# RWKV-7 recurrence and a SoLU block on one core: inverted blocks issued ahead of four loads, parts of an inverse moved behind evictions, the last store on two queues

## The chip, the cores and the metric

The kernel runs on one core of one Trainium2 chip. The metric is the device time of one execution in microseconds (us), as the median of seven runs. Engines: TensorE (PE; PEld are its weight loads), VectorE (DVE), ScalarE (ACT), GpSimd (POOL) and SyncE (SP), which here only issues DMAs. Each engine works through its instructions strictly in the order in which the program gives them.

## The reference

```python
B, H, S, D = 4, 8, 768, 40          # r, k, v, w, a, b: (B, H, S, D), float32
state = zeros(B, H, D, D)
for t in range(S):
    y[:, :, t] = einsum('bhd,bhde->bhe', r_t, state)
    Sa    = einsum('bhde,bhe->bhd', state, a_t)
    state = state * w_t[:, :, None, :] - einsum('bhd,bhe->bhde', Sa, b_t)
    state = state + einsum('bhd,bhe->bhde', v_t, k_t)
x = y.transpose(0, 2, 1, 3).reshape(B * S, H * D)      # 3072 x 320
h = x @ w_in                                           # w_in 320 x 1024, float64
solu = h * softmax(h)
out = (layernorm(solu) * g_ln) @ w_out                 # w_out 1024 x 320, float64
```

## The kernel before

**Tiling.** The sequence is cut into 12 rounds of 64 time steps (`L = 64`, `NCH = 12`). A round is one set of loads: for each of w, b, a, k, v and r two DMAs of 64 partitions with 16 runs of 160 bytes each. A round has two steps `i` (`N = 24` in all), each with two of the four batches and all eight heads. Within a step the recurrence is turned into matrix products over the 64 positions. This needs the inverse of a unit triangular 64 x 64 matrix for every batch and head.

**The inverse.** For the first four rounds (`FINE = 4`) only the 16 x 16 diagonal blocks are inverted by elimination; TensorE puts them together to 32 and 64. The blocks travel through DRAM so that every partition holds one block:
- `scatter(n)` (L424) writes the blocks of round n to DRAM with four DMAs of 512 runs of 128 bytes;
- `gather(n)` (L434) reads them back with two DMAs;
- `invert_fine(n)` is the elimination on VectorE: one step sets up u (L447, L448), fourteen steps are a product and a subtraction each (L456, L458; called pairs 1 to 14 here), the last copies u on ScalarE (L462) and writes it to DRAM with two DMAs (L464);
- `bring_inverse(n)` (L499) reads u back into the tile tinvT, two steps at a time, with four DMAs of 512 runs of 128 bytes;
- `solve(i)` transposes tinvT on VectorE (L598) and builds the larger inverse: py on TensorE, its eviction to `y_16` on VectorE (L602), pz on TensorE, evictions to tinvT on ScalarE (L613, or L610 for step 0), then py, y_mid, pz and L633 for the last doubling.

Step 0 takes another way: `solve(0)` doubles the blocks from 1 to 16 on TensorE, with L589 and the transpose L593 on VectorE and a copy on ScalarE (L592) at each doubling, while `invert(0)` works beside it for step 1.

**Other parts of a step.** `front(i)` makes decays and keys: the logarithm of w (L353), inv (L358), the products with b and k on GpSimd (L360), transposed a and b (L400, L401, L289) and the triangular matrix nt (L311). `attend(i)` makes psi and lamv; its fourth part transposes r (prT, L289). `recurrence(i)` makes pu, nuT, lamu, the output pyo and the next state sm; `readout(i)` makes x (L730). After a round, `repack` (L741 to L744) brings x into xT with twelve DMAs. From step 6 on, `hidden` and `output` compute the SoLU block for the step six behind; every second step ends in `store(n)` with two DMAs. `weights()` (W) brings in the matrices of the SoLU block piece by piece over GpSimd's queue (L228) and narrows them from 64-bit floats (the tile bits) on VectorE and ScalarE (L179 to L191).

**The order.** It is written out by hand. In `turns(order, ...)` each letter stands for the next part of one of these generators: f and g are fronts, r recurrence, a attend, s solve, I the inverse of the round to come, y readout, X repack, B the arrivals, W weights, L a later load, `*` a filler matmul. Where a letter I stands for several steps, a list says how many; for the step `i` that is `inverse_steps(i)`. `EARLY[1]` is the order of step 0 alone, `EARLY[0]` that of steps 1 to 5. Before the loop, two strings of letters cover the fronts of steps 0 to 3 and `solve(0)`.

**Queues.** Nearly all DMAs are issued by SyncE, one behind the other, and each may wait for the data it moves, for the readers of its target, and for the DMA that is eight places ahead of it. Between steps 0 and 1 the program issues, in this order: `scatter(2)`, k of round 3, r of round 1, and then, in the part B of step 1, `bring_inverse(1)` and `gather(2)`. k of round 3 is first read by GpSimd in the front of step 6, r of round 1 by prT in step 1.

```python
            if js and js[-1] % 2:
                scatter(js[-1] // 2)
            if i == 0:
                load(3, "k")
                load(1, "r")
            begin(i + 1)
```

Of the kernel before, what the change touches and what calls it, by code (L numbers as in the profile page):

```python
# [19 lines left out]
L = 64  # L20
# [36 lines left out]
def doubling_masks():  # L57

    s, t = np.arange(P)[:, None] % L, np.arange(L)[None, :]
    return np.concatenate([(s // (2 * b) == t // (2 * b)) & (s & b == 0) & (t & b != 0) for b in (1, 2, 4, 8)],  # L60
                          1).astype(np.float32)
# [3 lines left out]
def kernel(  # L65
# [28 lines left out]
    nc = tc.nc  # L94
# [4 lines left out]
    NCH = S // L  # L99
# [176 lines left out]
    def half(p):  # L276
        return slice(64 * p, 64 * p + 64)
# [41 lines left out]
    of_round = [dict() for _ in range(NCH)]  # L319

    def load(n, *names, by=(nc.sync, nc.sync)):

        if n >= NCH:
            return
        d = of_round[n]
        for name in names:
            ap = dict(w=w, b=b, a=a, k=k, v=v, r=r)[name]
            if name in "vr":
                d[name] = dict(v=v_t, r=r_t)[name][n % 2]
                to = d[name].rearrange("q s h c -> q (s h) c")[:, :, 0:D]  # L330
            else:
                d[name] = raw.tile([P, 2, H, D], FP32, tag="raw_" + name, name="raw_" + name)
                to = d[name].rearrange("q s h c -> q (s h) c")
            for c in range(2):
                by[c].dma_start(out=to[half(c)], in_=ap[2 * c:2 * c + 2, :, n * L:(n + 1) * L, :]  # L335
                                  .rearrange("b h t d -> t (b h) d"))
# [39 lines left out]
    def quarter(q):  # L376
        return slice(Q * q, Q * q + Q)

    def homes(q, steps=slice(0, 2)):

        return slice((q * 2 + steps.start) * H, (q * 2 + steps.stop) * H)
# [36 lines left out]
    def scatter(n):  # L418

        d = of_round[n]  # L420
        d["blocks"] = dram.tile([64, Q, Q], FP32, tag="blk_dram", name="blk_dram")
        nt = d["nt"].rearrange("q s p g t -> q (s p g) t")
        for q in range(4):
            nc.sync.dma_start(out=d["blocks"][homes(q)].rearrange("h s t -> s h t"),  # L424
                              in_=nt[quarter(q), :, quarter(q % 2)])

    def gather(n):


        if n < FINE:  # L430
            R = Q // 2
            nb = of_round[n]["nb"] = two.tile([P, R, R], FP32, tag="blk", name="blk", bufs=2)
            for z in range(2):
                nc.sync.dma_start(out=nb[half(z)],  # L434
                                  in_=of_round[n]["blocks"][:, R * z:R * z + R, R * z:R * z + R])
            return
        nb = of_round[n]["nb"] = two.tile([P, Q, Q], FP32, tag="blk", name="blk", bufs=2)
        for p in range(2):
            nc.sync.dma_start(out=nb[half(p)], in_=of_round[n]["blocks"])
# [55 lines left out]
    def bring_inverse(n, steps=slice(0, 2)):  # L495

        u = of_round[n]["u"]
        for q in range(4):
            nc.sync.dma_start(  # L499
                out=ti_t[quarter(q), steps, :, :, quarter(q % 2)].rearrange("s z p g t -> s (z p g) t"),  # L500
                in_=u[homes(q, steps)].rearrange("h s t -> s h t"))
# [307 lines left out]
    def store(n):  # L809
        rows = out.rearrange("(b s) d -> s b d", b=B)[n * L:(n + 1) * L]  # L810
        for c in range(2):
            nc.sync.dma_start(out=rows[:, 2 * c:2 * c + 2, :], in_=of_round[n]["osb"][half(c)])

    def steps(part, n):
        for _ in range(n):
            if part:
                next(part, None)

    def turns(order, more, **parts):

        for x in order.split():
            n = more.get(x, 1)
            steps(parts.get(x), n.pop(0) if isinstance(n, list) else n)

    def fronts(i):

        return [j for j in ((4, 5) if i == 0 else (i + AHEAD,)) if j < N]

    EARLY = ("r r a r B W f I r r W I W s y r X W a I s f L W a I a s W f I a f W s I a f W s f W",
             "r r a r W f r r W g W s y r W a f g L W a I a s f g W a I s f g W I s a f g W I s f g W I")  # L830
    STEADY = "r b r a r B f b b o r o I o r o s y o r X I o h a f L a s a h f a I h f s h f h a f h"
    CENTRE = "r r a r f o I r o r o s y o r X I o h a f L a s a h I f s a h I f s h f s h I a f h"
    LATE = "r b r r a B b b r o o I o r o s y o r X I o h a L a s a h a I h s h h a h"
# [4 lines left out]
    def begin(i):  # L838
        for j in fronts(i):
            front_of[j] = front(j)  # L840
            steps(front_of[j], 1)

    def inverses():
        for n in range(1, NCH):
            yield from invert(n)

    def inverse_steps(i):

        if i == 0:
            return [5, 5, 5, 1, 0]  # L850
        if i == LAG - 1:
            return [0, 0, 4, 4, 3, 3]
        if i == LAG:
            return [3, 3, 4, 4, 4]
        if i < LAG:
            return [0, 0, 2, 2, 2, 2] if i % 2 else [3, 3, 1, 1, 0, 0]
        return [0, 7, 7] if i % 2 else [6, 7, 5]

    def warm(n, x):

        for _ in range(n):
            nc.tensor.matmul(idle[:, 0:x.shape[1]], lhsT=x[:, 0:P], rhs=x, start=True, stop=True)

    def fillers():
        while True:
            warm(1, sm_t[0].rearrange("q c g d -> q (c g d)")[:, 0:256])
            yield
# [5 lines left out]
    def arrivals(i):  # L873

        n = (i + 1) // 2
        if n < NCH:
            bring_inverse(n)
        if n + 1 < NCH:
            gather(n + 1)
        yield  # L880

    def later(n, *names):
# [3 lines left out]
    with tc.manual_schedule():  # L886
        both = (nc.sync, nc.scalar)
        load(0, "w", "b", "a", by=both)
        nc.scalar.dma_start(out=masks, in_=nc.inline_tensor(doubling_masks(), name="masks").ap())
        load(0, "k", "v")  # L890
        load(1, "w", "a", "b")
        warm(3, sm_t[0].rearrange("q c g d -> q (c g d)"))
        f, g, at, inv, so, ws = front(0), front(1), attend(0), invert(0), solve(0), weights()
        turns("f g f g f f g g f f f g g s g a", {}, f=f, g=g, s=so, a=at)
        f, g, warmer = front(2), front(3), fillers()
        scatter(0)
        load(0, "r")
        gather(0)
        load(1, "k")
        load(2, "w")  # L900
        turns("f g s f s * g a s f I s I f a s I g I s I g a I", dict(I=[2, 3, 3, 3, 3, 99]), f=f, g=g, s=so, a=at, I=inv,
              **{"*": warmer})
        load(2, "a", "b")
        bring_inverse(0, slice(1, 2))
        turns("s f W s * f a s a g s g f g W W", {}, f=f, g=g, s=so, a=at, W=ws, **{"*": warmer})
        scatter(1)
        load(2, "k")
        gather(1)
        load(1, "v")
        begin(0)  # L910
        inv = inverses()
        after, before = None, None
        for i in range(N):
            m, more, js = i - LAG, i + 1 < N, fronts(i)
            now = hidden(m) if m >= 0 else None
            parts = dict(r=recurrence(i), y=readout(i), I=inv, W=ws, h=now, b=after, o=before)
            if i == LAG:
                steps(ws, 99)
                parts["o"] = centre()
                steps(parts["o"], 1)  # L920
            parts.update(zip("fg", (front_of[j] for j in js)))
            if more:
                parts.update(a=attend(i + 1), s=solve(i + 1))
            if i % 2 == 0:
                load((i + 6) // 2, "w", "a")
                parts["L"] = later((i + 6) // 2, *("bk" if i else "b"))
            else:
                parts["X"] = repacked(i // 2)
                parts["B"] = arrivals(i)
            order = EARLY[len(js) - 1] if i < LAG else CENTRE if i == LAG else STEADY if js else LATE  # L930
            turns(order, dict(I=inverse_steps(i)), **parts)
            if i % 2:
                load((i + 3) // 2, "v", "r")
            if js and js[-1] % 2:
                scatter(js[-1] // 2)
            if i == 0:
                load(3, "k")
                load(1, "r")
            begin(i + 1)
            after, before = now, output(m) if m >= 0 else None  # L940
        for m in range(N - LAG, N):
            now = hidden(m)
            turns("b h h h h h o o h b b o o o o", {}, h=now, b=after, o=before)
            after, before = now, output(m)
        turns("b b b o o o o o o", {}, b=after, o=before)
# [30 lines left out]
```

## Time and profile before

| | |
|---|---|
| median of seven runs | 675.37 us (672.97 to 681.46) |
| profiled execution, its own time | 672.97 us |
| its span, first to last instruction | 670.9 us |
| mean granted TensorE clock | 0.976 |
| TensorE busy | 608.9 us (91% of the span) |
| VectorE busy | 443.0 us (66%) |
| ScalarE busy | 275.4 us (41%) |
| GpSimd busy | 119.5 us (18%) |
| bytes moved by DMA | 53.74 MB in 238155 packets |

All times below are counted in us from the start of the span. The profile is of one execution, the fastest of the seven. A busy TensorE is not TensorE at its peak, as the ends of its matmuls are modelled. "[1.71 <-issue]" behind an instruction is the idle time of its engine just before it and what ended it; such a cause is inferred, and a wait for several things is put down to one of them. "SPq" is SyncE issuing a DMA, "DMA x<-y" a transfer that is waited for.

### The profile page before, as it was taken

The page shows a single profiled execution, that of the slowest core. Times are in us where ns is not written, and L with a number is a line of the kernel's source. Part 1 is how long each engine was busy: PE and PEld are TensorE (multiplying, and loading weights), DVE is VectorE, ACT ScalarE, POOL GpSimd, SP SyncE. Part 2 cuts the span into 40 slices and gives each one's busy share as a digit, 9 for nine tenths or more (in the row PEclk, how much of TensorE's full clock was granted, in tenths as well). Part 3 has the DMA queues.
Part 4 walks back from the last instruction along what each step waited for, and adds up shares of the span by engine and source line. Part 5 has one row for each costly group of instructions (what it writes and reads, how often), then busy time and mean ns, then how long its engine had stood idle before and what let it go on. Part 6 is the DMA issues. An engine that isn't in the chain of part 4 may idle for free.

```text
span 670.9 us, 28595 instructions
## 1 busy us (share of the span) xinstructions
PE 608.9 (91%) x12579; PEld 428.9 (64%) x12579; DVE 443.0 (66%) x1203; ACT 275.4 (41%) x663; POOL 119.5 (18%) x219
## 2 busy tenths in 40 slices
PE   7877677888789999999999999999999999999996
PEld 4666565776666677677667767676765666555554
DVE  4459567684796786886876876976967844323423
ACT  3254545565435344434534443452443334412312
POOL 4424313322221121122112112111200100000000
PEclk9798879998999999999999999999999999999999
DMA  9769649474373546454453643654234120000000
GB/s 154 111 147 153 124 81 161 81 135 98 82 118 50 94 80 109 66 100 88 78 96 81 90 84 77 85 94 93 39 67 81 24 41 19 21 24 21 20 21 20
DMA packets 238155, 53.74 MB, mean 80 GB/s; under 512 B 227400, under 2 KB 235344, under 8 KB 238032
## 3 DMA queue, kind: packets, MB, share of 16 engines
q1 hardware_dynamic: 232928, 45.80, 40.2%
q0 software_dynamic: 1696, 5.25, 3.0%
q8 instruction: 99, 1.62, 1.1%
q10 hardware_dynamic: 3408, 0.87, 0.9%
q14 instruction: 24, 0.20, 0.1%
HBM read 36.95 MB, written 10.22 MB: 70 GB/s over the span
## 4 chain that ended last, share of the span: by engine, by line
PE 66%; DVE 13%; ACT 6%; SPq 5%; issue 5%; DMA 3%; ACTq 1%; DVEq 0%
PE po L799 16%; PE h L754 13%; PE pyo L723 4%; PE pcx L370 3%; PE plnT L794 3%; PE py L547 3%; PE pz L547 3%; PE pcum L357 2%; DVE prod L486 2%; DVE u L488 2%; PE plamv L308 2%; SPq L335 2%; PE ppsi L308 2%; DVE nmax L764 2%; PE plamu L308 2%
## 5 line engine op out<-in xcount | busy, mean ns | idle before, releaser
L754 PE MATMUL h<-w_in,xT 128*128 128x512 f32 (+1 forms) x288 | 125.0, 624 | 0.0
L799 PE MATMUL po<-w,lnT 128*128 128x320 f32 x384 | 115.9, 440 | 3.2 <-ACT lnT L795 3.2
L799 PEld LDWEIGHTS po<-w,lnT 128*128 128x128 f32 x384 | 68.3, 190 | 29.2 <-ACT lnT L795 5.8
L488 DVE TENSOR_TENSOR u<-u,prod 128x30 f32<-128x30 f32 (+7 forms) x240 | 66.6, 278 | 8.2
L486 DVE TENSOR_TENSOR prod<-blk,u 128x30 f32<-128x30 f32 (+7 forms) x240 | 65.7, 274 | 7.2 <-DMA blk<-blk_dram 0.3
L764 DVE TENSOR_REDUCE nmax<-h 128x1 f32<-128x1024 f32 x24 | 29.3, 1221 | 52.5 <-PE h L754 52.5
L360 POOL TENSOR_TENSOR kx<-raw_b,inv 128x320 f32<-128x320 f32 x24 | 21.0, 876 | 233.5 <-ACT inv L358 220.9
L754 PEld LDWEIGHTS h<-w_in,xT 128*128 128x128 f32 (+1 forms) x288 | 38.0, 188 | 29.7 <-issue 27.7
L804 ACT ACTIVATE osb<-po,rs 128x320 f32<-128x320 f32 x24 | 12.6, 527 | 98.9 <-PE po L799 82.2
L795 ACT COPY lnT<-plnT 128x512 f32<-128x512 f32 x48 | 27.0, 587 | 41.1 <-PE plnT L794 41.0
L786 POOL TENSOR_TENSOR rs<-c,mhalf 128x1 f32<-128x1 f32 x24 | 13.2, 549 | 151.7 <-DVE c L785 150.6
L311 DVE TENSOR_TENSOR lamv<-plamv,cst 128x512 f32<-128x512 f32 x24 | 16.6, 690 | 31.8 <-PE plamv L308 30.8
L771 DVE TENSOR_TENSOR e<-h,e 128x1024 f32<-128x1024 f32 x24 | 29.4, 1224 | 10.0 <-ACT e L768 9.4
L547 PE MATMUL py<-tinv,nt 32*32 32x32 f32 x1280 | 24.0, 196 | 13.1 <-DVE tinv L598 11.6
L768 ACT ACTIVATE e<-h,nmax 128x1024 f32<-128x1024 f32 x24 | 26.8, 1115 | 20.6 <-DVE nmax L764 15.3
L633 ACT ACTIVATE tinvT<-pz 32x256 f32<-32x256 f32 x48 | 17.9, 373 | 40.9 <-PE pz L547 40.6
L370 PE MATMUL pcx<-cst,lw 128*128 128x132 f32 x192 | 31.7, 290 | 2.8 <-DVE y L602 1.5
L370 PEld LDWEIGHTS pcx<-cst,lw 128*128 128x128 f32 x192 | 26.4, 192 | 11.2 <-ACT y_mid L629 3.4
L372 ACT ACTIVATE kx<-pcx 128x264 f32<-128x264 f32 x48 | 18.8, 392 | 33.1 <-PE pcx L370 32.8
L709 POOL TENSOR_TENSOR sm<-tot,fac 128x320 f32<-128x320 f32 x20 | 14.8, 740 | 96.7 <-DVE tot L708 63.0
L547 PEld LDWEIGHTS py<-tinv,nt 32*32 32x32 f32 x1280 | 20.2, 110 | 17.8 <-issue 13.9
L776 DVE BATCH_NORM_STATS2 bs<-e 128x6 f32<-128x512 f32 x48 | 30.8, 684 | 0.6
(139 smaller groups left out, 1173.0 us busy)
## 6 DMA issues: line engine op xcount, KB each, us to landing
blk<-blk_dram SPq DMA_DIRECT2D x16, 256.0 KB
raw_k<-in_k_dram SPq DMA_DIRECT2D x24, 160.0 KB
v<-in_v_dram SPq DMA_DIRECT2D x24, 160.0 KB
r<-in_r_dram SPq DMA_DIRECT2D x24, 160.0 KB
out_dram<-osb SPq DMA_DIRECT2D x24, 160.0 KB
raw_w<-in_w_dram SPq DMA_DIRECT2D x23, 160.0 KB
raw_b<-in_b_dram SPq DMA_DIRECT2D x23, 160.0 KB
raw_a<-in_a_dram SPq DMA_DIRECT2D x23, 160.0 KB
```

The source lines that it names most:

```text
L308: nc.tensor.matmul(t[half(c ^ p * cross), p, g * L:(g + 1) * L], lhsT=lhs[half(p), g, half(c)], rhs=rhs[half(p), g, half(c)], start=True, ...
L370: nc.tensor.matmul(t[:, g * 132:g * 132 + 132], lhsT=pair(lw, 2 * j + g), rhs=cst[:, lo:lo + 132], start=True, stop=True)
L486: nc.vector.tensor_tensor(out=t, in0=nb[:, j:j + 1, j + 1:Q].to_broadcast([P, rows, m]), in1=u[:, 0:rows, j:j + 1].to_broadcast([P, rows, ...
L488: nc.vector.tensor_tensor(out=u[:, 0:rows, j + 1:Q], in0=u[:, 0:rows, j + 1:Q], in1=t, op=ALU.subtract)
L547: nc.tensor.matmul(t[quarter(out), c:c + Q], lhsT=lhs(p, g), rhs=rhs(p, g), start=True, stop=True)
L723: nc.tensor.matmul(t[half(p), c, g * W:g * W + used], lhsT=kb[half(c), j, 2 * g + p, :], rhs=lam[half(c), h % 2, h // 2, 0:used], start=i ...
L754: nc.tensor.matmul(h[:, j * 512:j * 512 + 512], lhsT=of_round[i // 2]["xT"][rows, kt, i % 2 * P:i % 2 * P + P], rhs=w_in[rows, 4 if kt == ...
L764: nc.vector.tensor_reduce(out=nmax, in_=h, axis=AX.X, op=ALU.max, negate=True)
L771: nc.vector.tensor_tensor(out=q, in0=h, in1=e, op=ALU.mult)
L776: nc.vector.bn_stats(out=bs[:, j], in_=q[:, j * 512:j * 512 + 512])
L795: nc.scalar.copy(out=lnT[:, fs.start:fs.stop].rearrange("p f t -> p (f t)"), in_=t)
L799: nc.tensor.matmul(o[:, 0:DM], lhsT=lnT[:, f, :], rhs=w2[:, f, :], start=f == 0, stop=f == NF - 1)
```

## The change

Five edits:
- In `arrivals` and the loop, `load(3, "k")` and `load(1, "r")` leave their place behind `scatter(2)`. In step 1 SyncE now issues `bring_inverse(1)`, k of round 3, `gather(2)` and r of round 1, in this order.
- In the first of the two strings of letters before the loop, the parts I (the inverse of round 0) are placed anew among the parts s, and the eighth s moves from the start of the second string to the end of the first, ahead of the last I. On VectorE, the transpose that ends the second doubling then comes ahead of the setting up of u and pair 1, the one that ends the third comes after pair 7 in place of pair 10, and L602 comes ahead of pair 14 but behind pairs 8 to 13.
- In `EARLY[1]`, one s goes ahead of I: L602 for step 1 comes ahead of the setting up of u of round 1.
- `inverse_steps(0)` gives 4 and 6 steps to the first two I in place of 5 and 5.
- Of the two DMAs of the last `store`, the second is issued by ScalarE.

On TensorE and GpSimd the order of the instructions is the same in both kernels. On ScalarE only the DMA at the end is added.

```diff
     def store(n):
         rows = out.rearrange("(b s) d -> s b d", b=B)[n * L:(n + 1) * L]
         for c in range(2):
-            nc.sync.dma_start(out=rows[:, 2 * c:2 * c + 2, :], in_=of_round[n]["osb"][half(c)])
+            (nc.scalar if c and n == NCH - 1 else nc.sync).dma_start(out=rows[:, 2 * c:2 * c + 2, :], in_=of_round[n]["osb"][half(c)])
...
     EARLY = ("r r a r B W f I r r W I W s y r X W a I s f L W a I a s W f I a f W s I a f W s f W",
-             "r r a r W f r r W g W s y r W a f g L W a I a s f g W a I s f g W I s a f g W I s f g W I")
+             "r r a r W f r r W g W s y r W a f g L W a a s I f g W a I s f g W I s a f g W I s f g W I")
...
     def inverse_steps(i):
         if i == 0:
-            return [5, 5, 5, 1, 0]
+            return [4, 6, 5, 1, 0]
...
     def arrivals(i):
         n = (i + 1) // 2
         if n < NCH:
             bring_inverse(n)
+        if i == 1:
+            load(3, "k")
         if n + 1 < NCH:
             gather(n + 1)
+        if i == 1:
+            load(1, "r")
         yield
...
-        turns("f g s f s * g a s f I s I f a s I g I s I g a I", dict(I=[2, 3, 3, 3, 3, 99]), f=f, g=g, s=so, a=at, I=inv,
+        turns("f g s f s * g a s f s I f a s I g I s I I g a s I", dict(I=[2, 3, 3, 3, 3, 99]), f=f, g=g, s=so, a=at, I=inv,
               **{"*": warmer})
         load(2, "a", "b")
         bring_inverse(0, slice(1, 2))
-        turns("s f W s * f a s a g s g f g W W", {}, f=f, g=g, s=so, a=at, W=ws, **{"*": warmer})
+        turns("f W s * f a s a g s g f g W W", {}, f=f, g=g, s=so, a=at, W=ws, **{"*": warmer})
...
             if js and js[-1] % 2:
                 scatter(js[-1] // 2)
-            if i == 0:
-                load(3, "k")
-                load(1, "r")
             begin(i + 1)
```

## The prediction

> **What bounds the kernel now.** The page came first. It names TensorE, but a busy share of 91% says little about the start, so the chain of waits was read next, in pieces.
>
> ```profile
> PE 608.9 (91%) x12579; PEld 428.9 (64%) x12579; DVE 443.0 (66%) x1203; ACT 275.4 (41%) x663; POOL 119.5 (18%) x219
> PE 66%; DVE 13%; ACT 6%; SPq 5%; issue 5%; DMA 3%; ACTq 1%; DVEq 0%
> ```
>
> From 120 us on the chain runs along TensorE and its evictions in program order, with no instruction that the diff touches until the last store. What the early steps gain or lose should therefore arrive at the end undiminished. Three early places and the tail remain. The chain from 70 us (start, duration, what):
>
> ```profile
> 75.14 0.48 SPq L424
> ...
> 77.08 2.01 SPq L335
> ...
> 79.13 1.02 SPq L335
> ...
> 80.67 2.01 SPq L499
> ...
> 83.27 1.11 SPq L499
> ...
> 84.42 2.37 DMA tinvT<-u_dram
> ...
> 86.91 0.71 DVE tinv L598
> ```
>
> Here the end is set by SyncE's queue: scatter of round 2 (L424), loads of k of round 3 and r of round 1 (L335), and only then the inverted blocks (L499), whose landing starts the transpose L598. TensorE's timeline shows the price:
>
> ```profile
> 77.61 0.66 PE L289 MATMUL pvT<-cst,v 128*128 128x128 f32 x4
> 87.77 1.08 PE L547 MATMUL py<-tinv,nt 32*32 32x32 f32 x64 [9.50 <-DVE tinv L598]
> ...
> 91.02 1.11 PE L289 MATMUL prT<-cst,r 128*128 128x128 f32 x4
> ```
>
> 9.50 us idle; 3.25 us later prT reads r, one of the loads that the change puts behind. The second place, first TensorE, then VectorE:
>
> ```profile
> 58.75 0.69 PE L308 MATMUL plamv<-rT,vT 64*64 64x64 f32 x32
> 61.16 1.01 PE L547 MATMUL pz<-tinvT,y 32*32 32x32 f32 x62 [1.71 <-issue]
> ```
>
> ```profile
> 58.71 0.28 DVE L447 TENSOR_SCALAR u<-blk 128x256 f32<-128x256 f32 x1
> ...
> 60.71 0.35 DVE L602 SCALAR_TENSOR_TENSOR y<-py,cst 128x128 f32<-128x128 f32 x1
> ```
>
> The gap is called issue, but pz reads y of L602, which ends at 61.06. Its input py was done at 56.9; five steps of the inverse (from L447) stand ahead of it. The third place is alike:
>
> ```profile
> 35.91 0.44 DVE L593 STREAM_TRANSPOSE y_mid<-tinv 128x256 f32<-128x256 f32 x1
> ...
> 37.96 0.18 DVE L458 TENSOR_TENSOR u<-u,prod 128x14 f32<-128x14 f32 x1
> 38.05 0.34 DVE L602 SCALAR_TENSOR_TENSOR y<-py,cst 128x128 f32<-128x128 f32 x1
> ```
>
> ```profile
> 38.45 0.75 PE L547 MATMUL pz<-y_mid,y 32*32 32x32 f32 x64 [1.18 <-DVE y L602]
> ```
>
> VectorE works without a pause from 31.93 to 38.4 and TensorE waits for it.
>
> **Third place (20 to 45 us), inverse of round 0.** The new order takes three multiply-subtract pairs from the free time before psi (VectorE idles 30.75 to 31.25 today, and would idle from 30.2) and puts them after 32.27. Before L602 then stand pairs 2 to 13 in place of 5 to 14: pairs 2, 3, 4 added (0.40 + 0.46 + 0.46 us by their spacing at 29.45 to 30.77), pair 14 taken away (0.40). L602 is 0.9 later. The copies of u on ScalarE (0.83 at 38.17) stand ahead of the copies of tinvT (L610) and wait for pair 14, now behind L602: by 39.8 against 38.17, and L610 from 40.6 against 39.24. The chain through L615 to py (40.98) loses 1.4. Bounds: -0.7 (the transpose L593, now ahead of three pairs, had waited 0.75 after its copy at 35.16, and this is all that could be won) and +1.7. I take +1.4, since no idle time of VectorE is left to absorb the pairs.
>
> A wider TensorE gap may also cost clock. It grows from 1.18 to about 2.1 us. The granted clock (the column ahead of the last two) after the 1.71 us gap above:
>
> ```profile
> 60.00:62.00 2.00, 0.84 (x67) 0.88 (x69) 1.86 (x8) 0.00 (x0) 0.00 (x0) 0.82 1.11 205
> 62.00:64.00 2.00, 2.00 (x51) 1.61 (x39) 1.83 (x8) 0.90 (x4) 0.54 (x1) 0.50 1.15 164
> ```
>
> It stays at half until 71.5; after the other gap of this size (1.74 us at 18.6) it is half from 20.3 to 27.1. These changes, and those at 81.7 and 92.0, lie multiples of 3.41 us apart. Four paT transposes take 1.09 us at half clock and 0.63 to 0.81 at full. So a drop here is possible: two windows of 3.4 us at a rate of 1/1.55 lose 2.4 us. It needs the gap to lie well inside a window, so it stays a rival. The Trainium skill ("TensorE: Matmul & The Clock Gate", HAM oscillation) warns of idle gaps above some 3.4 us; by that rule no gap of 2.1 us would cost anything, but the rows show a fall after 1.7. By the rule the term stays +1.4, by the rows it may be +3.8.
>
> **Second place (50 to 75 us).** L602 moves from behind five steps to right after psi (ending 58.7), so pz starts when plamv ends, at 59.45: 1.71 sooner. The steps lose nothing, for VectorE is busy from 50 to 70.3 in either order. It then idles 1.47 until pnt, and TensorE's lead removes that: nt comes 1.3 to 1.5 sooner. The u copy (71.07, from pairs done at 69.2) and the tinvT copies behind it (71.91, for pu at 72.72) come up to 2.0 sooner. Bounds -1.3 and -2.0; I take -1.7.
>
> **First place (73 to 92 us).** On SyncE the four issues of L499 move ahead of four loads, and the two gather issues (L434) ahead of the two of r. The issue total is unchanged; k is two DMAs, r two. From the scatter's end (75.63): u had landed by 77.04 at the latest (r's load waits for the DMA eight places before it, which is u's, and started then without delay), pu has read the old blocks by 73.5, so the first issue starts at once. Four issues take 1.95 us in the rounds after (124.60, 167.86) and 4.24 here, behind a full queue; then 2.5 us from the last issue's end (84.38) to the transpose (86.91). That gives 80.1 to 82.4; I take 80.5, as nothing is queued ahead: 6.4 sooner than 86.91.
>
> Then r is late. SyncE goes on from 77.7: k 1.4, gather 1.3, r 1.4 to 3.1, so r is issued by 82 to 83.6. Its landing by packets: blocks, k, gather and r are 2048 each (64 partitions x 16 runs, twice; 32 x 16, four times), 8192 in all. The packets by stretch are 796 from 76.5 to 78, 1316 and 1130 in the two stretches of 2 us to 82 while weights flow, then 1640 to 2112 per 2 us. With the first stretch free of its pause, some 1500 + 2446 move by 82; the other 4246 take 4.0 to 5.2 us: r lands at 86 to 87.2, prT at 86.5. By issue times alone: 82 + 2.5 = 84.5 to 83.6 + 5.8 = 89.4 (5.8 is from k's issue end 77.04 to its reader on GpSimd, 82.82). prT moves from 91.02 to 86.5: -4.5. Bounds -6.4 (r in time) and +2.5 (last rival).
>
> What else waits: k lands near 85, 2 us later; GpSimd's product (82.82 now) holds its queue, whose next issue (90.84) moves to about 86.3, so it is just covered, else up to 0.5 us. Gather lands by 83, ahead of L447. Repack's twelve issues start at 83.6 behind r, not when x is ready (82): 9.4 us of work for a reader many steps on, so nothing.
>
> **Tail.**
>
> ```profile
> 665.68 0.53 ACT L804 ACTIVATE osb<-po,rs 128x320 f32<-128x320 f32 x1 [3.87 <-PE po L799]
> 666.24 1.25 SPq L812 DMA_DIRECT2D out_dram<-osb  x2
> ```
>
> Two issues of 0.62 one behind the other become two side by side (ScalarE's early issues took 0.61 to 0.79): -0.6, bounds -0.6 and +0.2; the landing, 3.4 us to the span's end, stays.
>
> **Sum.** +1.4 - 1.7 - 4.5 - 0.6 = -5.4. The profiled execution took 672.97 us, 670.9 of it span, and was the fastest of seven: it would become 667.6. Against their median of 675.37 the same difference gives 670.0, 0.8% less.
>
> **Rivals.**
> - *r is not late and the clock holds.* If the packets of r run beside the others, prT follows the transpose: -6.4, with +0.9 at the third place and -2.0 at the second: -8.1, 667.3. For it: DMA pauses at 76.5 and 84.5. Against: four transfers of equal size, r last.
> - *The clock falls at the third place.* +2.4 on the forecast: -3.0, 672.4. For it: the two gaps of 1.7 us. Against: the gap of 1.18 us leaves it at 1.00 today.
> - *The wait only changes its name.* r lands at 89.4: the first place gives -1.6, the sum -2.5, 672.9. The change then does little of what it says.
> - *r becomes the bound and it is slower.* SyncE's queue with its slowest rows (4.24 for blocks, 2 x 1.70 for k, 1.32, 3.07, then 5.8 to land) brings r at 93.5: +2.5, in sum +1.6, 677.0. It decides from a landing after 91.9. Against: those rows were measured behind the loads that now come later.
>
> **How the numbers follow.** Chances: forecast 0.44, r in time 0.30, clock 0.14, renamed wait 0.06, slower 0.06. A measurement of this kernel tells about 1% (6.8 us) from no change. Faster by that means under 668.6: most of the first rival and a quarter of the forecast's spread, 0.37. Slower by 1% needs more than 682.1, beyond every case: 0.04. The range goes from 664.5 (the first rival and the 2.4 us between the median and the fastest run) to 675.0 (past clock and renamed wait).
>
> **What would show it.** In the changed profile: L499 issues right after L424; L598 near 80 less the shift of the stages before; TensorE's 9.5 us gap split in two, the second ended by prT or r; the gap before pz gone near 59; L602 of the third place about 1 us later; two stores side by side. I am wrong if prT does not move by 3 us or more, or if the second place gains nothing.

## The result, and the profile after

The changed kernel takes 679.15 us (median of 27 runs, 674.58 to 684.35); the kernel before, over all its 64 runs, 679.79 us (672.97 to 685.29). The ratio is 1.0009, 95% interval 0.9989 to 1.0029: no difference. The prediction (670.0, range 664.5 to 675.0) was wrong. Its starting point was low too: the seven runs known then had a median of 675.37, 4.4 us under the later one; the difference forecast, -5.4 us, is what counts below.

The profiled execution took 674.77 us, its span is 673.0 us and its mean granted clock 0.974 (before: 672.97, 670.9, 0.976). First two lines of the page: busy time of each engine, and the chain that ended last by engine.

```profile
PE 611.0 (91%) x12579; PEld 432.3 (64%) x12579; DVE 441.9 (66%) x1203; ACT 275.6 (41%) x663; POOL 119.0 (18%) x219
PE 66%; DVE 14%; ACT 6%; DMA 5%; issue 4%; SPq 4%; ACTq 1%; DVEq 0%
```

DMA went from 3% to 5% of the chain, SyncE's issues from 5% to 4%. The chain from 76 us, as start, duration, what, shows why:

```profile
76.13 0.14 SPq L499
...
78.13 1.68 SPq L335
...
80.62 1.36 SPq L434
...
83.61 1.37 SPq L335
...
85.03 4.35 DMA r<-in_r_dram
...
89.51 1.09 PE prT L289 x4
```

SyncE does what the diff says: inverted blocks (L499), k, gather, r. In this chain nothing waits for the blocks any more; it now runs through the whole queue to its last member, r, which is 4.35 us on the way. The four groups whole (start, time to issue):

```profile
75.92 2.16 SPq L499 DMA_DIRECT2D tinvT<-u_dram  x4
78.13 2.40 SPq L335 DMA_DIRECT2D raw_k<-in_k_dram  x2
80.62 2.94 SPq L434 DMA_DIRECT2D blk<-blk_dram  x2
83.61 2.97 SPq L335 DMA_DIRECT2D r<-in_r_dram  x2
```

TensorE in the first place (start, duration, line, operation; in brackets the idle time ahead):

```profile
78.77 0.66 PE L289 MATMUL pvT<-cst,v 128*128 128x128 f32 x4
81.75 0.74 PE L547 MATMUL py<-tinv,nt 32*32 32x32 f32 x64 [2.31 <-DVE tinv L598]
...
89.51 1.09 PE L289 MATMUL prT<-cst,r 128*128 128x128 f32 x4 [5.75 <-DMA r<-in_r_dram]
...
103.49 1.19 PE L684 MATMUL pu<-tinvT,x 64*64 64x64 f32 x32
```

The 9.50 us gap became 2.31 and 5.75. py starts 6.02 earlier than in the profile before (87.77), prT 1.51 earlier (91.02), but pu of step 2 later (103.49 against 101.95). The work from prT to pu is the same in both kernels and took 13.98 us in place of 10.93. The granted clock (ahead of the last two columns; the first numbers are the stretch) says what happened to it:

```profile
84.00:86.00 2.00, 0.00 (x0) 0.00 (x0) 0.00 (x0) 0.26 (x1) 0.13 (x1) 1.00 0.76 75
86.00:88.00 2.00, 0.00 (x0) 0.00 (x0) 0.29 (x1) 0.00 (x0) 0.72 (x1) 0.98 0.67 114
88.00:90.00 2.00, 0.49 (x3) 0.52 (x4) 1.92 (x8) 0.00 (x0) 0.40 (x1) 0.50 0.41 102
...
102.00:104.00 2.00, 2.00 (x27) 1.67 (x28) 1.90 (x8) 0.94 (x2) 0.55 (x1) 0.50 0.58 85
104.00:106.00 2.00, 2.00 (x51) 1.42 (x49) 0.70 (x4) 1.24 (x6) 0.00 (x0) 0.76 0.88 177
```

TensorE stands still through the first two rows; the clock halves about 87.9 and stays at half to 105.0, though TensorE has no gap after 89.5. Before the change it was half from 81.7 to 92.0, mostly while nothing ran.

Second place, TensorE, then VectorE with both places:

```profile
57.97 0.69 PE L308 MATMUL plamv<-rT,vT 64*64 64x64 f32 x32
58.60 0.72 PE L547 MATMUL pz<-tinvT,y 32*32 32x32 f32 x62
...
65.91 1.06 PE L547 MATMUL py<-tinv,nt 32*32 32x32 f32 x32 [3.67 <-DVE kx L401]
```

```profile
56.92 0.35 DVE L602 SCALAR_TENSOR_TENSOR y<-py,cst 128x128 f32<-128x128 f32 x1
58.87 0.49 DVE L447 TENSOR_SCALAR u<-blk 128x256 f32<-128x256 f32 x1 [1.60 <-DMA blk<-blk_dram]
...
80.89 0.71 DVE L598 STREAM_TRANSPOSE tinv<-tinvT 128x512 f32<-128x512 f32 x1 [1.59 <-DMA tinvT<-u_dram]
...
87.66 0.29 DVE L447 TENSOR_SCALAR u<-blk 128x256 f32<-128x256 f32 x1 [4.70 <-DMA blk<-blk_dram]
```

L602 comes right after psi and the gap ahead of pz is gone. But py of the same step waits 3.67 us for the products L401 and starts at 65.91, where before it started at 65.80: the wait has moved on from pz to py. The third place, VectorE and TensorE:

```profile
29.05 0.68 DVE L311 TENSOR_TENSOR psi<-ppsi,cst 128x512 f32<-128x512 f32 x1
...
34.16 0.44 DVE L593 STREAM_TRANSPOSE y_mid<-tinv 128x256 f32<-128x256 f32 x1
...
37.36 0.34 DVE L602 SCALAR_TENSOR_TENSOR y<-py,cst 128x128 f32<-128x128 f32 x1
```

psi starts 2.2 us earlier than before (31.25), L602 only 0.69 earlier (38.05): the three added pairs are there, 8.31 us from psi to L602 in place of 6.80. The gap of TensorE behind L602, 1.18 us before, is 0.43 us. The tail, two issues side by side:

```profile
668.07 0.53 ACT L804 ACTIVATE osb<-po,rs 128x320 f32<-128x320 f32 x1 [3.87 <-PE po L799]
668.63 0.59 SPq L812 DMA_DIRECT2D out_dram<-osb  x1
668.63 0.67 ACTq L812 DMA_DIRECT2D out_dram<-osb  x1
```

From that osb to the end of the span: 4.9 us, before 5.2.

The stretches of all the kernels below, each from one profile (us). "Second" runs from pvT of step 1 to the end of the last eviction nt (L311); the next two columns run from there to prT of step 2 and from prT to pu. Times to compare kernels by are the ratios of their runs, since these stretches also carry what the clock did in that one execution.

| kernel | second | nt to prT | prT to pu | last two |
|---|---|---|---|---|
| before | 20.47 | 17.91 | 10.93 | 28.84 |
| changed | 20.99 | 15.95 | 13.98 | 29.93 |
| queue_alone | 20.73 | 15.39 | 13.98 | 29.37 |
| order_alone | 20.86 | 17.61 | 11.40 | 29.01 |
| loads_early | 19.86 | 14.62 | 10.75 | 25.37 |
| loads_only | 20.69 | 12.01 | 10.88 | 22.89 |
| loads_pairs | 21.51 | 14.08 | 11.38 | 25.46 |
| filled | 21.02 | 20.64 | 10.45 | 31.09 |
| filled_few | 19.73 | 15.55 | 10.59 | 26.14 |
| first_order | 20.56 | 15.96 | 12.51 | 28.47 |
| pairs_behind | 19.21 | 17.79 | 13.99 | 31.78 |
| r_next | 20.28 | 11.99 | 14.27 | 26.26 |

### The profile page after: what moved, and what is told of

Its sections match the earlier page's. It is cut to its first block, busy times and chain, and to the rows that moved or that the text cites. A ratio compares the mean times of both kernels' runs of the same rounds, so it can differ in the third digit from the quotient of the medians.

```text
span 673.0 us, 28599 instructions
## 1 busy us (share of the span) xinstructions
PE 611.0 (91%) x12579; PEld 432.3 (64%) x12579; DVE 441.9 (66%) x1203; ACT 275.6 (41%) x663; POOL 119.0 (18%) x219
## 4 chain that ended last, share of the span: by engine, by line
PE 66%; DVE 14%; ACT 6%; DMA 5%; issue 4%; SPq 4%; ACTq 1%; DVEq 0%
PE po L799 16%; PE h L754 13%; PE pyo L723 4%; PE plnT L794 3%; PE pz L547 3%; PE pcx L370 3%; PE py L547 2%; DVE prod L486 2%; PE plamv L308 2%; DVE u L488 2%; PE pcum L357 2%; DMA blk<-blk_dram 2%; DVE nmax L764 2%; PE plamu L308 2%; PE ppsi L308 2%
## 5 line engine op out<-in xcount | busy, mean ns | idle before, releaser
L360 POOL TENSOR_TENSOR kx<-raw_b,inv 128x320 f32<-128x320 f32 x24 | 21.0, 876 | 234.8 <-ACT inv L358 201.4
L311 DVE TENSOR_TENSOR lamv<-plamv,cst 128x512 f32<-128x512 f32 x24 | 16.6, 690 | 33.6 <-PE plamv L308 33.5
L771 DVE TENSOR_TENSOR e<-h,e 128x1024 f32<-128x1024 f32 x24 | 29.4, 1224 | 10.2 <-ACT e L768 9.7
L370 PEld LDWEIGHTS pcx<-cst,lw 128*128 128x128 f32 x192 | 26.8, 195 | 10.5 <-ACT y_mid L629 3.4
L730 DVE TENSOR_TENSOR x<-pyo,kx 128x512 f32<-128x512 f32 x24 | 16.2, 673 | 20.8 <-PE pyo L723 20.8
```

What stands on the lines that cost most here:

```text
L370: nc.tensor.matmul(t[:, g * 132:g * 132 + 132], lhsT=pair(lw, 2 * j + g), rhs=cst[:, lo:lo + 132], start=True, stop=True)
L771: nc.vector.tensor_tensor(out=q, in0=h, in1=e, op=ALU.mult)
```

## The experiments

Each has 12 timed runs beside the kernel before on the same chip; the ratio is to that kernel, with its 95% interval.

**queue_alone: only SyncE's order.** The kernel before, with this edit:

```diff
+        if i == 1:
+            load(3, "k")
         if n + 1 < NCH:
             gather(n + 1)
+        if i == 1:
+            load(1, "r")
...
-            if i == 0:
-                load(3, "k")
-                load(1, "r")
```

> The kernel before with the one edit to SyncE's queue (inverted blocks, k, gather, r). Theory G (given back): the blocks come about 6 us sooner, but the gathered blocks and r, now behind them, come late: prT moves by less than 2 us, and the half clock after it takes the rest. Expected within 0.3% of before (2 us). Rival O (the order): the queue edit does gain its 4.5 us, and the two edits to the order of the inverse lose them. Expected 3.5 to 5 us faster than before (ratio 0.9925 to 0.995).

679.43 us, ratio 0.9997 [0.9970, 1.0025]. The part that was to bring 4.5 us brings nothing by itself. TensorE in its first place:

```profile
82.46 1.08 PE L547 MATMUL py<-tinv,nt 32*32 32x32 f32 x64 [4.38 <-DVE tinv L598]
...
88.27 1.08 PE L289 MATMUL prT<-cst,r 128*128 128x128 f32 x4 [2.49 <-DMA r<-in_r_dram]
...
102.25 0.90 PE L684 MATMUL pu<-tinvT,x 64*64 64x64 f32 x32
```

The same picture as in the changed kernel: r ends the wait, and 13.98 us from prT to pu, with the clock at half from 82.1 to 102.6. From the last nt to pu it needs 29.37 us, the kernel before 28.84.

**order_alone: only the strings of letters.** The kernel before with the two first strings, `EARLY[1]` and `[4, 6, 5, 1, 0]` of the changed one.

> The kernel before with the edits to the two strings, EARLY[1] and inverse_steps(0), and nothing else. Theory G: the gap before pz goes, but TensorE then waits at py for L401, which stands behind six pairs; the two places cancel, within 0.3% of before. Rival O: 3 to 5 us slower than before (ratio 1.0045 to 1.0075).

679.62 us, ratio 1.0006 [0.9973, 1.0040]. The second and third places together are worth nothing that can be measured. The forecast for the two was -0.3 us in sum (+1.4 and -1.7), so these times speak against neither term alone; the profiles have to. The second place takes 20.86 us here, where before has 20.47.

**loads_early: r and k out of the burst.** The changed kernel, but the two loads go out in step 0 behind b of round 3, where SyncE stands idle until u is ready (65.1 to 71.5 in the profile before):

```diff
-        if i == 1:
-            load(3, "k")
...
-        if i == 1:
-            load(1, "r")
...
     def later(n, *names):
         load(n, *names)
+        if n == 3:
+            load(1, "r")
+            load(3, "k")
```

> The changed kernel, but r of round 1 and k of round 3 are issued in step 0, right after b of round 3, where SyncE waits some 4 us for u and the DMA engines stand still. The inverted blocks then have neither ahead nor behind them. Theory G: L598 as early as in the changed kernel, gathered blocks 4 us earlier, prT right behind ppsi near 84 in place of 89.5; 5 to 8 us faster than before (ratio 0.988 to 0.993). Rival O: r was not what cost the gain; less than 2 us from the changed kernel.

676.88 us, ratio 0.9956 [0.9935, 0.9977]: faster than the changed kernel, but by less than was expected. prT follows the transposes without a wait for r and prT to pu takes 10.75 us. What ends the wait now is the trip of u through DRAM: L598 waits 5.46 us for tinvT.

**loads_only: the same two loads moved in the kernel before**, with no edit of the change.

> The kernel before, of which only r of round 1 and k of round 3 are moved: into step 0, right after b of round 3. No edit of the change is in it. Theory G: what held the kernel was the place of these two loads, ahead of the blocks as well as behind them; the order edits of the change add nothing or cost 1 to 2 us at the third place (its gap let the clock fall in 2 of 4 profiles with the new order, in none of 2 with the old). Expected ratio to before 0.991 to 0.995, not behind loads_early (0.9956). Rival O2: the new order of the inverse gains 1.7 us at the second place, and this kernel lacks it: 0.9965 to 0.999.

676.84 us, ratio 0.9940 [0.9902, 0.9978], as expected. TensorE, then SyncE's queue (start, duration, line):

```profile
83.92 0.93 PE L547 MATMUL py<-tinv,nt 32*32 32x32 f32 x64 [3.71 <-DVE tinv L598]
...
87.02 0.93 PE L289 MATMUL prT<-cst,r 128*128 128x128 f32 x4
...
97.90 0.75 PE L684 MATMUL pu<-tinvT,x 64*64 64x64 f32 x32 [1.55 <-DVE x L665]
```

```profile
66.69 1.96 SPq L335 DMA_DIRECT2D r<-in_r_dram  x2
68.74 2.91 SPq L335 DMA_DIRECT2D raw_k<-in_k_dram  x2
73.19 1.13 SPq L464 DMA_DIRECT2D u_dram<-u  x2
75.04 2.18 SPq L424 DMA_DIRECT2D blk_dram<-nt  x4
77.40 1.95 SPq L499 DMA_DIRECT2D tinvT<-u_dram  x4
```

Both loads are issued before u is ready, so the blocks still go right behind the scatter, and prT stands 3.1 us behind py with no gap. The last two columns of the table sum to 22.89 us, 5.95 less than before. So the wait at L598 that the prediction read was real, and worth about what it said; it is won by taking the loads out of the queue, not by changing places with them. The gain in the time of whole runs is 0.6%, 4 us; whether the other 2 us are lost later stays open. It is read from the ratio and not from this one profile: its span is 675.2 us, since from pu to the last osb it took 572.1 us, where the profiles of before and changed show 563.7 and 564.6 and queue_alone 567.2. No edit touches that stretch, and over the twelve kernels of the table single executions range from 561.4 to 572.1 us in it.

**r_next: r ahead of the gather.** The changed kernel with r and k exchanged (blocks, r, gather, k):

```diff
         if i == 1:
-            load(3, "k")
+            load(1, "r")
         if n + 1 < NCH:
             gather(n + 1)
         if i == 1:
-            load(1, "r")
+            load(3, "k")
```

> The changed kernel with the same four places on SyncE's queue, but r of round 1 right behind the inverted blocks, then the gathered blocks, then k. If r's place alone makes the wait, r lands 3 to 4 us sooner, prT follows 12 to 13 us after nt in place of 16, and with the shorter gap the clock recovers sooner: 3 to 5 us faster than the changed kernel (0.993 to 0.997). Rival: the DMA engines are full from the scatter on, the gathered blocks then hold VectorE at L447 and pz behind it, and the gain is under 1 us.

677.70 us, ratio 0.9964 [0.9929, 0.9999]: within what was expected, some 3 us below the changed kernel's 1.0009, though the two intervals overlap. r lands earlier and prT starts 11.99 us behind nt in place of 15.95, as expected. But then the gathered blocks are late (L447 starts at 86.95 after a wait of 4.42 us), L602 stands behind them on VectorE, and so does pz:

```profile
85.25 0.63 PE L289 MATMUL prT<-cst,r 128*128 128x128 f32 x4 [1.93 <-DMA r<-in_r_dram]
...
88.03 1.08 PE L547 MATMUL pz<-tinvT,y 32*32 32x32 f32 x64 [2.15 <-issue]
```

The next wait is that for the gathered blocks, which are late in both kernels (L447 starts at 87.66 in the changed one). From nt to pu it takes 26.26 us in place of 29.93. k, now last, holds GpSimd until 88.79 and ends no wait of TensorE that this profile shows.

**filled: matmuls in the gap.** The changed kernel with 14 matmuls on constants, 128x256, ahead of prT in step 1, to keep the clock up:

```diff
+    def fill():
+        warm(14, cst[:, 0:256])
+        yield
...
+            if i == 1:
+                order = order.replace("L W a I a s", "L W a I * a s")
...
+                parts["*"] = fill()
```

> The changed kernel with 14 filler matmuls of 128 x 256 ahead of prT in step 1, some 5 us of work in the gap in which TensorE waits for r. The loads are as late as before. Theory G: the clock does not fall to half near 88, and the 15 us of work behind the gap run at full clock; 2 to 4 us faster than the changed kernel (ratio to before 0.994 to 0.998). Rival C (the clock does not matter there, since VectorE sets the pace): within 1 us of the changed kernel, or slower if the fillers end after r has landed.

677.53 us, ratio 0.9981 [0.9950, 1.0013]. Too many: the trace shows 28 records in 7.63 us, which hold prT back to 95.41, after r has landed. From there to pu, at full clock, it takes 10.45 us.

**filled_few: half as many.** The same with `warm(7, ...)`.

> The changed kernel with 7 filler matmuls (14 in filled, which ended long after r had landed) ahead of prT in step 1: 3.8 us of work that ends before r lands, so that nothing waits for them. From prT to pu of step 2 took 14.0 us in all three profiles with r behind the blocks (the changed kernel, queue_alone, pairs_behind), at half clock throughout, and 10.5 to 11.4 us in the other five. Clock theory: prT at the same place, 16 us after nt, and 10.5 to 11.4 us from there to pu: 3 us faster than the changed kernel (ratio to before 0.995 to 0.998). Rival: the 14 us come from what lands late (gathered blocks, k), and the fillers change nothing: 14 us again, within 1 us of the changed kernel.

677.74 us, ratio 0.9975 [0.9935, 1.0014].

```profile
85.47 3.29 PE L862 MATMUL idle<-cst 128*128 128x256 f32 x14
90.50 0.63 PE L289 MATMUL prT<-cst,r 128*128 128x128 f32 x4 [1.75 <-DMA r<-in_r_dram]
...
101.09 0.75 PE L684 MATMUL pu<-tinvT,x 64*64 64x64 f32 x32 [1.55 <-DVE x L665]
```

```profile
88.00:90.00 2.00, 0.76 (x4) 0.33 (x2) 1.17 (x7) 0.00 (x0) 0.00 (x0) 1.00 0.59 106
90.00:92.00 2.00, 1.50 (x90) 1.36 (x92) 1.88 (x7) 0.59 (x1) 0.58 (x1) 1.00 0.22 60
```

The fillers end before r lands, prT starts as far behind nt as in the changed kernel (15.55 against 15.95), the clock stays at 1.00, and prT to pu takes 10.59 us. Blocks and k are as late against prT as in the changed kernel (L447 starts 1.76 us ahead of it, there 1.85; GpSimd's product with k 3.54, there 3.64), so the rival is out. This is the direct evidence that the clock, and not another wait, made these 3 us in the changed kernel's profile. In the time of whole runs the gain is not resolved: the interval holds 1.

**first_order: the third place undone.** The changed kernel with the two first strings of the kernel before.

> The changed kernel with the two strings of letters ahead of the loop as before: the third place undone, all else kept. If the new order there costs the 1.4 us that the prediction put on it (or more by the clock), 1 to 2 us faster than the changed kernel (ratio to before 0.997 to 0.999). If the new order gains instead, slower than the changed kernel by 1 us or more (1.002 and up).

679.22 us, ratio 1.0000 [0.9969, 1.0031], against 1.0009 with the new strings. No difference is to be seen, but the interval is 2.1 us wide to either side, so that a loss of 1.4 us can't be told from none by the times. In the profiles the last py of step 0's inverse starts at 40.69 here and at 40.63 in the changed kernel.

**pairs_behind: the wait of the second place.** The changed kernel with both products L401 of step 0 ahead of the next six pairs:

```diff
-"... g W s y r W a f g L W a a s I f g W a I s f g W I s a f g W I s f g W I"
+"... g W s y r W a f g L W a a s I f g W a s f g I W I s a f g W I s f g W I"
```

> The changed kernel with the two L401 of step 0 ahead of the next six pairs of the inverse, all else kept. PSUM theory: the 3.67 us wait at py goes, nt and the scatter of round 2 come 2 to 3 us sooner; 2 to 3 us faster than the changed kernel (0.996 to 0.998). Rival: the time is set by r and the gathered blocks, whose loads start from the scatter, so the gain arrives in full; or by VectorE, and it is within 1 us of the changed kernel.

678.73 us, ratio 1.0003 [0.9969, 1.0036].

```profile
63.44 0.69 PE L547 MATMUL py<-tinv,nt 32*32 32x32 f32 x32 [0.90 <-DVE kx L401]
...
83.70 1.08 PE L547 MATMUL py<-tinv,nt 32*32 32x32 f32 x64 [4.69 <-DVE tinv L598]
...
89.59 1.09 PE L289 MATMUL prT<-cst,r 128*128 128x128 f32 x4 [2.58 <-DMA r<-in_r_dram]
```

The wait ahead of py falls from 3.67 to 0.90, and py starts 10.85 us behind pvT of step 1 in place of 13.34, with the clock full up to 64 in both. So L401 behind the pairs was what held py. The second place falls from 20.99 to 19.21 us, but the clock was at half for 3.4 us of it here and for 9.6 in the changed kernel, so that not all of the 1.8 us is shown to be the order's. The gain ends at the first place: blocks and r come no sooner, prT stands at 89.59 and the clock is half from 81.4 on.

**loads_pairs: the loads and the pairs together.** The kernel before, with the loads of loads_only, L602 ahead, both L401 ahead of the six pairs, and `[4, 6, 5, 1, 0]`.

> loads_only with a new order at the second place: L602 ahead of the inverse as in the change, and in addition the two L401 of step 0 ahead of the next six pairs. In the changed kernel TensorE waited 3.67 us at py for L401, since the two buffers of the PSUM tag bank were held by paT. If that wait is what ate the 1.71 us, py comes near 62.5 in place of 65.9 and the stage between the pvT of steps 1 and 2 shrinks from 25 to 26 us to 22 to 23: 2 to 3 us faster than loads_only (0.987 to 0.991). Rival: VectorE sets the pace there, and the wait only moves on to u: within 1 us of loads_only.

673.56 us, ratio 0.9918 [0.9885, 0.9951]: with the next one the lowest ratio here, faster than both kernels of the change, though by a little less than was expected. Its profile doesn't explain a gain over loads_only: its second place took 21.51 us there, with a half clock through part of it, and py started 12.84 us behind pvT. That the pairs add to the loads is therefore not shown: the times alone say it, with overlapping intervals (0.9940 and 0.9918).

**loads_pairs_fill: with fillers and the tail.** loads_pairs with six fillers behind pvT of step 1 and the last store on two queues.

> loads_pairs with 6 filler matmuls behind pvT of step 1, where TensorE still waits 4 to 6 us for the inverted blocks, and the last store on two queues (0.3 us, from the profiles so far). Clock theory: py, pcx, ppsi and prT run at full clock behind the wait, 1 to 2 us faster than loads_pairs (ratio to before 0.988 to 0.991). Rival: the fillers only take the place of a wait that the clock survives in most runs; within 1 us of loads_pairs (0.9918).

674.16 us, ratio 0.9915 [0.9886, 0.9943]: the same as loads_pairs. Once r is no longer late, more fillers and the tail add nothing that can be told.

## Why the prediction was wrong, step by step

**First place, forecast -4.5, and this term failed.** The reading of the wait was right: with the four issues ahead, L598 starts at 80.89 (forecast 80.5) in place of 86.91. What failed is the landing of r, and in it the time that SyncE needs to issue what now stands ahead of r. The prediction charged 1.4 us for k, 1.3 for the gather and 1.4 to 3.1 for r, and so had r issued by 82 to 83.6. k took 2.40, the gather 2.94, r 2.97, and the issue of r ended at 86.58. In the profile before, the same four groups were

```profile
75.67 1.37 SPq L335 DMA_DIRECT2D raw_k<-in_k_dram  x2
77.08 3.07 SPq L335 DMA_DIRECT2D r<-in_r_dram  x2
80.67 4.24 SPq L499 DMA_DIRECT2D tinvT<-u_dram  x4
84.95 1.32 SPq L434 DMA_DIRECT2D blk<-blk_dram  x2
```

10.00 us in sum, after the change 10.47, where the prediction's prices add up to 6.1 to 7.8. The prediction itself wrote that the issue total is unchanged; by that, the issue of the last group ends near 86 in either order. But it took k and gather at their short times, 1.37 and 1.32, in places of the queue where these had not been measured, and the blocks near 1.95, from later rounds. Why the same pair of DMAs takes 1.4 us to issue in one place and 2.4 in another no run here separates. In the five profiles with this order in which prT waits for r (the changed kernel, queue_alone, filled_few, first_order, pairs_behind) the four groups took 8.3 to 10.5 us, and prT starts 2.9 to 4.7 us behind the end of r's issue, 13.0 to 15.6 us behind the end of the scatter; the forecast for the last had 10.9 (86.5 less 75.63), and before it was 15.4. The packet count was too high as well, 2446 from 78 to 82 us where 1157 and 988 went through.

From the end of its issue r needed 2.8 us and landed at 89.4, the number that the prediction had put into its rival "the wait only changes its name". That the number fits so well is partly luck: the rival added 83.6 and 5.8, and neither part is right. prT moved by 1.51 us, not 4.5, which is the condition named there for being wrong.

**The term that was not in the sum: +3.0.** The prediction had the clock as a risk, but at the third place, for a gap of about 2 us. At the first place it split a gap of 9.5 us in two and took the clock for unchanged. Yet the new gap, 5.75 us, lies directly ahead of long gapless work, and that work then ran at half clock. In the profile before, half clock fell mostly on the gap itself. The stretch from prT to pu goes by how much of it ran at half clock: 10.45 and 10.59 us with none (filled, filled_few), 10.75 to 10.93 with 0.6 to 1.0 us (loads_early, loads_only, before), 11.38 and 11.40 with 2.2 and 2.3 (loads_pairs, order_alone), 12.51 with 6.4 (first_order), 13.98 to 13.99 with all of it (queue_alone, pairs_behind, the changed kernel). Only r_next stands apart, with a wait inside the stretch. Net of the first place in the profiles: -1.96 + 3.05, about +1.1 us.

**Second place, forecast -1.7, measured nothing.** The step that failed is "TensorE's lead removes that: nt comes 1.3 to 1.5 sooner". pz did start sooner, at 58.60 in place of 61.16. (Ahead of it psi came 1.84 us sooner, which is not the edit to `EARLY[1]`: L189 and L191 took 0.83 us on VectorE in place of 2.58; before, GpSimd's products with k, L360, ran at the same time.) But TensorE does not keep the lead. py takes a PSUM bank from the pool of two that paT uses too, and can't start before L401 has read paT; L401 stands behind the pairs, and so behind the same work of VectorE in either order. order_alone shows it with the slow L189 and L191 of before: py starts 13.30 us behind pvT of step 1, before 13.16. In the changed kernel it is 13.34, as VectorE, early there, waits 1.60 us for the gathered blocks at L447; filled_few, with no such wait, has 12.09. nt ends no sooner either (second place 20.99 us, before 20.47). pairs_behind, with L401 ahead of six pairs, has py at 10.85.

**Third place, forecast +1.4, measured nothing.** From psi to L602 the profile has 8.31 in place of 6.80 us: +1.5, where the pairs were to add 0.9. Not foreseen was that psi itself comes sooner. In the old order a transpose and then psi stand behind L447, and when the gathered blocks are late, both wait (3.33 us in loads_only, 3.29 in first_order; only 0.17 in the profile before, whose half clock from 20.3 to 27.1 hid it). The failed step is "no idle time of VectorE is left to absorb the pairs": the wait for the blocks is such time. L602 lands 0.69 earlier, not 0.9 later, and py behind it at 40.63, not 1.4 later than 40.98; first_order has 40.69. The rival "the clock falls at the third place" did not come to its price: the gap that was to grow to 2.1 us is 0.43, and between 20 and 52 us the mean clock was 0.95 after and 0.89 before. The clock was at half from 33.3 to 36.7, but near there also with the old strings in queue_alone, loads_only and first_order.

**Tail, forecast -0.6: -0.35.** Side by side, the issues took 0.59 and 0.67 us in place of 1.25 one behind the other, and the span ends 4.9 us after the start of the last osb in place of 5.2. An issue saved is not wholly a gain.

**The sum.** With the measured terms: 0.0 + 0.0 - 2.0 + 3.0 - 0.35, about +0.7 us, where -5.4 was forecast. The measured ratio of 1.0009 with its interval allows -0.7 to +2.0 us. That the two meet is partly luck, since the terms come from one execution of each kernel: its span grew by some 2 us, and besides these terms that has -0.07 up to pvT of step 1, +0.52 at the second place and +0.85 between pu and the tail, where the change touches nothing and single executions differ by more. Of the rivals, "the wait only changes its name" was the right one (0.06), and it stood at 672.9, as it still held the gains of the second place and of the tail and had no term for the clock. The lower end of the range was added up wrong (667.3 less 2.4 is 664.9, not 664.5); nothing hangs on it.

**On the clock rule.** The prediction weighed the Trainium skill ("TensorE: Matmul & The Clock Gate", HAM oscillation) against the trace. The 5.75 us gap agrees with its rule of idle gaps above some 3.4 us. The same page's Part 1 has about 3.4 us of sustained work bring the clock back; in the profile before 4.2 us did (87.8 to 92.0), but after the change 15.5 us without a gap, from 89.5 to 105.0, did not, and the measurement decides.

## What to carry to other kernels

When a DMA is moved ahead in one engine's queue, follow the transfers that it passes to their first readers: price the last of the queue by the issue time of the whole burst, not by the shortest time of each part. What gained clearly here was a place where the queue is idle (loads_only, 0.9940). Of the orders of the same burst, blocks, k, gather, r gained nothing (queue_alone, 0.9997); blocks, r, gather, k perhaps 2 us (r_next, 0.9964). When a long gap is split, ask what runs right behind the new gap, since that work pays if the clock falls there. When an eviction (a copy out of PSUM) is moved ahead of other work on an engine, find the next eviction behind that work and the matmul that needs its bank.

## What the runs showed of the hardware

- After two gaps in close order the clock stayed at half for 17.1 us (changed kernel), 20.5 (queue_alone), 23.9 (pairs_behind) and 13.6 us (first_order), while after one longer gap it was back after 10.2 us (before, 9.50 us gap; order_alone, 7.57 us gap). Close gaps alone don't decide it: r_next, with gaps of 2.48, 1.93 and 2.15 us, was back after 6.8 us. In the three longest cases TensorE worked without a pause on transposes, on 32x32 and 64x64 matmuls and a few of 128x132 for most of that time. Fourteen records of 128x256 matmuls in 3.29 us between the gaps of filled_few (2.56 and 1.75 us) were enough to hold it at 1.00. What of the work counts, size or kind, was not tried. The Trainium skill ("TensorE: Matmul & The Clock Gate", Part 4) says that transposes don't count as busy in the same way; no run here separates that.
- In the burst of small transfers after the change 1157 and 988 packets went through in the two stretches of 2 us from 78 us, while the weights flowed; 1605 and 1812 in the next two. r, issued last, needed 4.35 us to land from the start of its second issue on.
- The time to issue one and the same group of DMAs on SyncE varies: k of round 3 took 1.37 us in the profile before, 2.40 in the changed kernel and 1.39 in queue_alone, the four DMAs of the blocks 4.24, 2.16 and 3.40.
- Moving u through DRAM ends in a wait in every profile here: L598 waits at least 1.59 us for tinvT (changed kernel), and with r out of the way 3.00 us (loads_only) to 5.46 us (loads_early).
